# Keys and queries of steps 14 to 23: block transposes on VectorE and a pass through DRAM instead of TensorE transposes

## The chip, the cores and the metric

The kernel runs on one core of a Trainium2 chip. The core has five engines with a queue of their own, each of which works through its instructions in order: TensorE (PE in the profile; PEld is its weight load), VectorE (DVE), ScalarE (ACT), GpSimd (POOL) and SyncE (SP), which here only issues DMA transfers. ScalarE can issue DMA transfers too. An engine waits for another, or for a transfer, by a semaphore; while it waits, everything behind in its queue waits as well. The metric is the device time of one execution in microseconds (us), the median of several runs.

## The reference

A delta-rule attention over 4 batches, 8 heads, 768 tokens and head width 48 feeds a feed-forward block with a hard-swish. All inputs and the output are float32.

```python
k_n = k / (np.linalg.norm(k, axis=-1, keepdims=True) + 1e-06)
state = np.zeros((B, H, D, D), dtype=np.float32)
for t in range(S):
    kt, vt, bt = (k_n[:, :, t], v[:, :, t], beta[:, :, t, None])
    y[:, :, t] = np.einsum('bhd,bhde->bhe', q[:, :, t], state)
    v_old = np.einsum('bhde,bhd->bhe', state, kt)
    state = state + bt[:, :, :, None] * np.einsum('bhd,bhe->bhde', kt, vt - v_old)
...
x = np.ascontiguousarray(attn_out.transpose(0, 2, 1, 3)).reshape(B * S, H * D)
h = x @ w_in          # 3072 x 384 by 384 x 2048
g = h * np.clip(h + 3.0, 0.0, 6.0) / 6.0
return g @ w_out      # 3072 x 2048 by 2048 x 384
```

## The kernel before

The 768 tokens are cut into N = 24 steps of C = 32 tokens. In one step the four batches lie side by side on the 128 partitions (partition = 32 * batch + token), and the free dimension holds 8 heads of width 48, in some buffers padded to 64. Within a step the recurrence is solved as a triangular system: scores of keys against keys and queries (`sc`, L547), masked and scaled into `L` and `LB` (L558), an inverse of the triangular matrix worked out on VectorE for four steps at a time (`pr` and `A`, L759 and L764), and then the chain from step to step.

Two steps make a block of 256 tokens for the feed-forward. Its up and down products fill TensorE between the pieces of the recurrence. From block 5 on the up product is done with eleven partial products (`up_by_eleven`, L1066, its copies and sums at L1080, L1093, L1097, L1100, L1104 and L1107), before that plainly (L994, L1001, L1004). From block 2 on the down product is done with seven (`down_by_seven`, L1218, with sums of g on VectorE at L1204). In the part of the run that the change touches, odd steps are mostly filled with down products and even steps with up products.

The order is written by the program itself, in emission order for every engine. The first steps follow a list of words. From step 5 on a loop goes over steps t, each cut into 15 units u = 0 to 14. In each unit it calls the entry of `plan` for that unit, two key loads if there are any, one piece of the feed-forward (`units`), and as many instructions of `fill` (the inverse, the norms) as `room` allows; `room` subtracts from 1.65 us what VectorE has to do in that unit (`USED`, `CHAIN`). `take(gen)` advances a generator to its next bare `yield`.

Names that matter:

- `prep(t)` makes ready what the scores of step t need. GpSimd writes the normalised key into `kb` (L510). TensorE transposes four 128 x 128 pieces of it into PSUM (`pt`, L524) and ScalarE copies them into `KQ` (L532); the same for the query `qb`. Then come the 64 score matmuls (L547), and VectorE writes `L` and `LB` (L558). From t = 7 on the loop prepares `first_of` = t + 6: GpSimd's product is emitted at unit 13 of the step before (`later`), then the key's transposes at unit 1, the query's at unit 2, scores at unit 4, masks and `LB` at unit 5 (`now`).
- `KQ` holds for one step both operands with the head width on the partitions: head pair member e and width d on partition 64 * e + d, and in the free dimension the head pair and batch pair, four places y (key, query, query, key) and 32 tokens. There are NKQ = 6 of these buffers, 4 KB on each partition. A `KQ` is read by the scores and, six steps later, by the matmuls against the state (`ks`, L806).
- `chain(t)` is the recurrence: `ks` (L806) at unit 0, `R` (L901, L909), the product with the inverse (`pz`, L827), the update `su` (L938) and `py` (L827) at unit 8, the addition `y += py` (L863) and the new state (L956) at unit 9, and the transposes `yt` of y (L873) with ScalarE's copy into `xT` (L877) at unit 10. The up product of the block reads `xT`, after the sums at L1056 where it is done with eleven products.
- `load_q`, `load_k`, `load_v` issue four transfers of 48 KB on SyncE for one step; `to_dram` stores the output. Queries have NQB = 4 buffers, keys `kb` two.

Of the kernel before, what the change touches and what calls it, by code (L numbers as in the profile page):

```python
# [9 lines left out]
FP32 = mybir.dt.float32  # L10
# [34 lines left out]
def kernel(  # L45
# [49 lines left out]
    def rows(b):  # L95
        return slice(C * b, C * b + C)
# [24 lines left out]
    qbufs = [persist.tile([P, H, DP], FP32, name=f"qb{i}") for i in range(NQB)]  # L121
    bkbufs = [bkb_spare] + [
        persist.tile([P, H, DP], FP32, name=f"bkb{i}") for i in range(1, NBKB)
    ]
# [1 line left out]
    def bkb_of(t):  # L126
        return bkbufs[t if t < NBKB else 1 + (t - 1) % (NBKB - 1)]
# [3 lines left out]
    def tokens(ap, b, t):  # L131
        return ap[b, :, t * C : (t + 1) * C, :].rearrange("h t d -> t h d")
# [4 lines left out]
    def needs(*what):  # L137
        assert past.issuperset(what), (what, set(what) - past)
# [33 lines left out]

    def load_q(t, eng=nc.sync):
        if t < N:
            if t >= NQB:
                needs(("qT", t - NQB))
            elif t:
                needs(*pad(t))
            for b in range(B):
                eng.dma_start(out=qbufs[t % NQB][rows(b), :, 0:D], in_=tokens(q, b, t))  # L180
                if b == B - 1:
                    past.add(("q", t))
                yield
# [310 lines left out]
    def scaled(t):  # L494
        needs(("kb", t), *pad(t), *([("bkb", t - NKB)] if t >= NKB else []))
        if t >= NBKB:
            needs(("su", t - NBKB + 1))
        nc.gpsimd.tensor_tensor(
            out=bkb_of(t)[:, :, 0:D], in0=kbufs[t % NKB][:, :, 0:D],
            in1=beta_tok[:, t, 0:H].unsqueeze(2).to_broadcast([P, H, D]), op=ALU.mult,  # L500
        )
        past.add(("bkb", t))
        yield

    def prep(t, whole=True):

        g, i = group(t)
        kb, qb = kbufs[t % NKB], qbufs[t % NQB]
        needs(*([("bkb", t - NKB)] if t >= NKB else []), *(pad(t) if t < NKB and t else []))
        nc.gpsimd.tensor_tensor(  # L510
            out=kb[:, :, 0:D], in0=kfs[g][:, i],
            in1=invs.pop(t).unsqueeze(2).to_broadcast([P, H, D]), op=ALU.mult,
        )
        past.add(("kb", t))
        yield

        for j, src in enumerate((kb, qb)):
            if j == 1:
                needs(("q", t))
                past.add(("qT", t))  # L520
            ring("pm", NPM, ("pt", t, j))
            pt = psM.tile([128, NP, P], FP32, name="pt", tag=slot["pm"])
            for p in range(NP):
                nc.tensor.transpose(  # L524
                    pt[:, p, :], src[:, 2 * p : 2 * p + 2].rearrange("p e w -> p (e w)"), ident[:]
                )
            yield 1
            if j == 0:
                ring("KQ", NKQ, ("KQ", t))
                KQ = work.tile([128, NP * B // 2, 4, C], FP32, name="KQ", bufs=NKQ)  # L530
            read(("pt", t, j))
            nc.scalar.activation(  # L532
                out=KQ[:, :, 0:4:3, :] if j == 0 else KQ[:, :, 1:3, :],
                in_=pt[:].rearrange("q p (x y c) -> q (p x) y c", y=2, c=C), func=ACTF.Copy,
            )
            if whole and j == 0:
                drain(mask(t))
            yield
        ring("pc", NPC, ("sc", t))
        sc = psC.tile([P, 2, 512], FP32, name="sc", tag=slot["pc"])  # L540
        scv = sc[:, :, 0 : NP * 2 * C].rearrange("p e (a j w) -> p e a j w", a=NP, j=2)
        for p in range(NP):
# [24 lines left out]
        yield  # L567
# [219 lines left out]
    def chain(t, whole=True):  # L787
# [10 lines left out]
        def of_state():  # L798
            ph = [banks("ks", t, i) for i in range(2)]
            for p in range(NP):  # L800
                for b in (0, 2, 1, 3):
                    for e in range(2):
                        r = slice(DP * e, DP * e + DP)
# [622 lines left out]
    with tc.manual_schedule():  # L1426
# [11 lines left out]
        loads = iter(())  # L1438
        left = due = 0
        USED = {"up": 0.42, "eleven": 1.0, "down": 0.7}  # L1440
        CHAIN = {0: 0.45, 1: 0.75, 2: 0.75, 3: 0.4, 4: 0.4, 6: 0.5, 9: 0.8, 10: 0.6, 14: 0.2}
        for t in range(LS, N):
            g, i = group(t)
# [9 lines left out]
            if i == 2:  # L1453
# [12 lines left out]
                11: lambda: token_sums(t // CB),  # L1466
                13: lambda: take(later),
            }
            if behind:
                for u in (7, 8, 10, 11, 12, 13):  # L1470
                    plan[u] = lambda ch=plan.get(u): (ch and u < 13 and ch(), take(more))
                plan[14] = lambda: take(later)
            ready = (2, 0) if behind or i == 2 and t - LS == LA - LE else (1, 6)
            for u in range(NU):
                if u in plan:
                    plan[u]()
                take(loads, 2)
# [24 lines left out]
                left, due = max(left - int(due), 0), due - int(due)  # L1502
# [33 lines left out]
```

## Time and profile before

| what | value |
|---|---|
| median of 3 runs | 665.78 us (665.2 to 667.13) |
| profiled execution, its own time | 672.08 us |
| its span | 670.4 us |
| granted TensorE clock, mean | 0.985 |
| first `ks` of steps 7, 8 and 18, from the span's start | 214.84, 240.44, 493.37 us |
| transposes `pt` (L524) | 192 in 48 groups, 24 of key and 24 of query; the last at 472.8 us |
| copies into `KQ` (L532) | 48, 576 to 608 ns each |

How to read the lines that follow: the page gives busy time and share of each engine, then the chain of work that ended last. A row of the table by stretches gives the stretch in us, its length, the busy time of each engine with its number of instructions, the granted clock, the share of the DMA engines and GB/s. A row of the timeline gives start, length from the first start to the last end, engine, line, operation, tile written <- tiles read, shapes and count; in brackets the idle time before it and what ended it. A row of the groups gives the count, busy us and mean ns of one, and the idle time before. A row of the DMA issues gives the count, the size and the median time from issue to landing.

### The profile page before, as it was taken

Reading aid. Unit: us, or ns where it says so; the run is one execution under the profiler, and the core shown is the slowest. Engines: PE = TensorE matmul, PEld = TensorE weight load, DVE = VectorE, ACT = ScalarE, POOL = GpSimd, SP = SyncE. Lnnn points to the kernel's source line nnn. Section 1 sums busy time; section 2 is a strip of 40 time slices with the busy share of each in tenths; the row PEclk is TensorE's granted clock in tenths of the full one; section 3 lists DMA queues with packets and bytes.
Section 4 is the critical chain, followed back from the end, with each engine's and each line's share of the span. In section 5 each row is a group of like instructions: output and inputs, shape, how many; then the busy total and the mean of one; then the engine's idle time right before and its main releaser. Section 6 shows DMA issues by size and latency. Waiting matters only on the chain.

```text
span 670.4 us, 26330 instructions
## 1 busy us (share of the span) xinstructions
PE 636.9 (95%) x11544; PEld 568.6 (85%) x11544; DVE 487.2 (73%) x1146; ACT 272.8 (41%) x532; POOL 203.6 (30%) x320
## 2 busy tenths in 40 slices
PE   2768899999999999999999999999999999999997
PEld 2657786776688988988989999999999999999997
DVE  4889685899545777747879847988748988556354
ACT  5887568532142232232234234235244144153250
POOL 5531022002421031364155255055042141331330
PEclk9959899999999999999999999999999999999999
DMA  7888237302041030032030020020020020010000
GB/s 171 203 193 235 59 67 186 73 6 51 15 80 32 2 72 2 3 73 37 3 68 8 3 61 14 3 62 2 3 50 2 2 49 2 17 24 2 25 1 25
DMA packets 88499, 33.27 MB, mean 50 GB/s; under 512 B 80160, under 2 KB 83232, under 8 KB 88384
## 3 DMA queue, kind: packets, MB, share of 16 engines
q1 hardware_dynamic: 88128, 31.29, 20.7%
q8 instruction: 91, 1.49, 0.9%
q10 hardware_dynamic: 256, 0.30, 0.2%
q14 instruction: 24, 0.20, 0.1%
HBM read 26.84 MB, written 4.72 MB: 47 GB/s over the span
## 4 chain that ended last, share of the span: by engine, by line
PE 86%; DMA 5%; DVE 3%; SPq 2%; issue 1%; ACT 1%; POOL 0%; ACTq 0%; DVEq 0%; POOLq 0%
PE po L1218 28%; PE ph L1066 20%; PE ph L994 15%; PE po L1154 6%; PE ks L806 3%; PE su L938 3%; PE pz L827 3%; PE py L827 3%; PE pt L524 2%; PE sc L547 2%; DMA spare<-in_moe_w_in_dram 2%; DMA kf<-in_k_dram 1%; PE yt L873 1%; DMA w_out<-in_moe_w_in_dram 1%; PE pi L684 1%
## 5 line engine op out<-in xcount | busy, mean ns | idle before, releaser
L1066 PE MATMUL ph<-xT,w_in 128*128 128x128 f32 (+1 forms) x560 | 121.4, 321 | 0.8 <-ACT KQ L532 0.6
L994 PE MATMUL ph<-xT,w_in 128*128 128x256 f32 (+1 forms) x576 | 116.6, 351 | 2.9 <-DVE g L1004 2.1
L1218 PE MATMUL po<-w_out,g 128*128 128x192 f32 x640 | 110.6, 326 | 0.0
L994 PEld LDWEIGHTS ph<-xT,w_in 128*128 128x128 f32 x576 | 94.5, 192 | 15.8 <-DVE g L1004 2.9
L1218 PEld LDWEIGHTS po<-w_out,g 128*128 128x128 f32 x640 | 104.6, 190 | 0.5
L1066 PEld LDWEIGHTS ph<-xT,w_in 128*128 128x128 f32 x560 | 91.1, 191 | 6.0 <-ACT KQ L532 0.8
L1030 POOL TENSOR_TENSOR g<-g 128x256 f32<-128x256 f32 x112 | 68.0, 608 | 83.2 <-ACT g L1080 78.8
L1218 PE MATMUL po<-spare,g 128*128 128x192 f32 x480 | 86.7, 332 | 0.0
L1218 PEld LDWEIGHTS po<-spare,g 128*128 128x128 f32 x480 | 77.2, 190 | 1.8
L1001 ACT ACTIVATE g<-ph,halves 128x256 f32<-128x256 f32 (+1 forms) x96 | 41.3, 436 | 74.9 <-PE ph L994 74.8
L1080 ACT ACTIVATE g<-ph 128x512 f32<-128x512 f32 x56 | 33.4, 597 | 82.1 <-PE ph L1066 82.1
L1228 POOL TENSOR_TENSOR o<-o,u 128x192 f32<-128x192 f32 x18 | 13.2, 733 | 175.7 <-ACT o L1225 97.2
L1204 DVE TENSOR_TENSOR g<-g 128x512 f32<-128x512 f32 x80 | 55.6, 716 | 5.6 <-PE po L1218 5.6
L759 DVE TENSOR_TENSOR pr<-A 128x30 f32<-128x30 f32 (+9 forms) x150 | 57.4, 383 | 2.8
L764 DVE TENSOR_TENSOR A<-A,pr 128x30 f32<-128x30 f32 (+9 forms) x150 | 55.7, 371 | 3.7
L1004 DVE SCALAR_TENSOR_TENSOR g<-g,ph 128x256 f32<-128x256 f32 (+1 forms) x96 | 34.8, 371 | 31.7 <-ACT g L1001 31.4
L356 ACT ACTIVATE spare<-spare,places 128x768 uint16<-128x768 uint16 (+1 forms) x56 | 52.4, 942 | 2.7 <-DMA kf<-in_k_dram 1.5
L1093 DVE TENSOR_TENSOR g<-ph,g 128x256 f32<-128x256 f32 x56 | 23.5, 420 | 38.4 <-PE ph L1066 30.9
L1225 ACT ACTIVATE o<-po 128x192 f32<-128x192 f32 x40 | 13.2, 330 | 83.2 <-PE po L1218 79.6
L510 POOL TENSOR_TENSOR kb<-kf,inv 128x384 f32<-128x384 f32 x24 | 21.3, 891 | 78.8 <-issue 42.6
L1154 PE MATMUL po<-w_out,g 128*128 128x384 f32 x128 | 45.2, 491 | 0.0
L1107 DVE SCALAR_TENSOR_TENSOR g<-o,g 128x512 f32<-128x512 f32 x56 | 40.7, 726 | 5.9 <-ACT o L1104 5.9
(141 smaller groups left out, 1010.6 us busy)
## 6 DMA issues: line engine op xcount, KB each, us to landing
kf<-in_k_dram SPq DMA_DIRECT2D x96, 48.0 KB, 2.9
qb<-in_q_dram SPq DMA_DIRECT2D x96, 48.0 KB, 2.8
vf<-in_v_dram SPq DMA_DIRECT2D x96, 48.0 KB, 2.2
out_dram<-o SPq DMA_DIRECT2D x92, 48.0 KB, 1.6
spare<-in_moe_w_in_dram SPq DMA_DIRECT2D x4, 768.0 KB, 6.0
w_out<-in_moe_w_in_dram SPq DMA_DIRECT2D x4, 768.0 KB, 6.5
w_out<-in_moe_w_out_dram SPq DMA_DIRECT2D x4, 768.0 KB, 7.3
spare<-in_moe_w_out_dram SPq DMA_DIRECT2D x4, 768.0 KB, 5.7
```

Of the source, the lines that this page charges most:

```text
L356: nc.scalar.activation(out=z, in_=z if n else d.bitcast(I16)[:, :, :, 3], func=func, bias=places[:, n : n + 1], scale=scale,)
L759: nc.vector.tensor_tensor(out=pv, in0=A[:, j + 1 :, j].unsqueeze(2).to_broadcast([n, w, j]), in1=A[:, j, 0:j].unsqueeze(1).to_broadcast([n ...
L764: nc.vector.tensor_tensor(out=A[:, j + 1 :, 0:j], in0=A[:, j + 1 :, 0:j], in1=pv, op=ALU.subtract)
L827: nc.tensor.matmul(ps[rows(place(b)), D * h : D * h + D], lhsT=m(h)[rows(b)], rhs=z[rows(b), D * at(h) : D * at(h) + D], start=True, stop= ...
L994: nc.tensor.matmul(ph[:, cols], lhsT=w_in[:, s, f * 128 : (f + 1) * 128], rhs=xT[:, s, cols], start=(s == 0), stop=(s == NKT - 1),)
L1001: nc.scalar.activation(out=g, in_=ph, func=ACTF.Relu, bias=half, scale=1.0 / 6.0)
L1030: nc.gpsimd.tensor_tensor(out=out, in0=a, in1=b, op=op)
L1066: nc.tensor.matmul(ph[:, n], lhsT=w, rhs=x, start=start, stop=stop, skip_group_check=True)
L1107: nc.vector.scalar_tensor_tensor(out=g, in0=r, scalar=1.0, in1=g, op0=ALU.min, op1=ALU.mult)
L1154: nc.tensor.matmul(pos[c][:], lhsT=gs[blk, f // 2][:, f % 2, c * P : (c + 1) * P], rhs=w_out[:, f, :], start=(f == 0), stop=(f == NFC - 1),)
L1204: nc.vector.tensor_tensor(out=A(f, *out, 4), in0=A(f, *a, 4), in1=A(f, *b, 4), op=op)
L1218: nc.tensor.matmul(ps[n][:], lhsT=A(f - f % 2, *a)[:, f % 2], rhs=b[:, f], start=(f == 0), stop=(f == HF - 1),)
```

## The change

For the steps from TQ = LS + 2 * LE + 1 = 14 on, `prep` uses no TensorE. VectorE transposes the 128 x 384 query in blocks of 32 x 32 into a buffer `turned`; SyncE writes it with four transfers, one for each batch, into a tile `kq` in DRAM (384 rows of head and width; two such tiles). The key follows in the same way, through the same `turned`. Then ScalarE issues two transfers that read `kq` into `KQ`, one for the even and one for the odd heads, in runs of 1 KB. The scores and `ks` read 48 of the 64 partitions of each half.

`KQ` becomes a ring of fixed slots. Six are the buffers of before; step 14 and every seventh step after it use a slot cut from the area of the four query buffers, which also holds `turned` and the one query buffer of the late steps (`late_q`). A late query can therefore be loaded only after the query before it has been turned.

In the loop, GpSimd's product and the query's turn are emitted at unit 7 of the step before, the key's turn at unit 8, the reads into `KQ` at unit 12. The masks stay at unit 1, the scores at unit 4. The entries at units 2 and 6 no longer advance `prep`. `room` subtracts 0.6 us more in units 7 and 8.

```diff
+    TQ = LS + 2 * LE + 1
+    q_area = persist.tile([P, NQB * H * DP], FP32, name="qb")
...
+    KQW = 4 * C * NP * B // 2
+    late_kq = q_area[:, 0:KQW].rearrange("p (a y c) -> p a y c", y=4, c=C)
+    turned = q_area[:, KQW : KQW + H * D]
+    late_q = q_area[:, KQW + H * D : KQW + 2 * H * D].rearrange("p (h w) -> p h w", w=D)
+    early_kq = [
+        persist.tile([128, NP * B // 2, 4, C], FP32, name=f"KQ{i}") for i in range(NKQ)
+    ]
+
+    def kq_slot(t):
+        return t % NKQ if t < TQ else NKQ if t == TQ else kq_slot(t - NKQ - 1)
...
     def load_q(t, eng=nc.sync):
         if t < N:
-            if t >= NQB:
-                needs(("qT", t - NQB))
+            if t > TQ:
+                needs(("qT", t - 1))
+            elif t >= NQB:
+                needs(*(("qT", t - NQB + n) for n in range(2 if t == TQ else 1)))
...
+        def turn_by_blocks(j):
+            nc.vector.transpose(
+                out=turned, in_=(of_query if j else of_key)(t).rearrange("p h w -> p (h w)")
+            )
+            for b in range(B):
+                nc.sync.dma_start(
+                    out=kq[:, b // 2, (2 if j else 3) if b % 2 else j, :].rearrange(
+                        "(n r) c -> r n c", r=C
+                    ),
+                    in_=turned[rows(b)].rearrange("p (n c) -> p n c", c=C),
+                )
+
+        if t >= TQ:
+            kq = scratch.tile([H * D, B // 2, 4, C], FP32, name="kq", bufs=2)
+            needs(("q", t))
+            turn_by_blocks(1)
+            past.add(("qT", t))
+            yield
+            turn_by_blocks(0)
+            yield
+            KQ = kq_of(t)
...
+            for e in range(2):
+                nc.scalar.dma_start(
+                    out=KQ[DP * e : DP * e + D].rearrange("d (p x) y c -> d p (x y c)", p=NP),
+                    in_=kq[:].rearrange("(p e d) x y c -> e d p (x y c)", e=2, d=D)[e],
+                )
+            yield
+            drain(mask(t))
+        yield
+
+        for j, src in enumerate((kb, qb) if t < TQ else ()):
...
-                    r = slice(DP * e, DP * e + DP)
+                    r = slice(DP * e, DP * e + (DP if t < TQ else D))
...
+        TURN = {7: 0.6, 8: 0.6}
...
+            if first_of >= TQ:
+                plan[2] = lambda: (take(ch), take(gens["q"], 4))
+                plan[6] = lambda: None
+            if first_of + 1 >= TQ:
+                plan[7] = lambda: take(later)
+                plan[8] = lambda: (take(ch), take(later))
+                plan[12] = lambda: take(later)
+                plan[13] = lambda: None
...
+            turns = TURN if first_of + 1 >= TQ else {}
...
-                room = max(1.65 - USED[mode["of"]] - CHAIN.get(u, 0), 0.15) / mode["mean"]
+                room = max(1.65 - USED[mode["of"]] - CHAIN.get(u, 0) - turns.get(u, 0), 0.15) / mode["mean"]
```

More of the change, by code (lines that the diff above doesn't have):

```diff
@@ L120, with kq_of, of_key, of_query @@
     kbufs = [persist.tile([P, H, DP], FP32, name=f"kb{i}") for i in range(NKB)]
-    qbufs = [persist.tile([P, H, DP], FP32, name=f"qb{i}") for i in range(NQB)]
+    TQ = LS + 2 * LE + 1
+    q_area = persist.tile([P, NQB * H * DP], FP32, name="qb")
+    qbufs = [
+        q_area[:, i * H * DP : (i + 1) * H * DP].rearrange("p (h w) -> p h w", w=DP)
+        for i in range(NQB)
+    ]
[5 more added lines that the diff above has]
+        persist.tile([128, NP * B // 2, 4, C], FP32, name=f"KQ{i}") for i in range(NKQ)
+    ]
+    def kq_slot(t):
+        return t % NKQ if t < TQ else NKQ if t == TQ else kq_slot(t - NKQ - 1)
+    def kq_of(t):
+        i = kq_slot(t)
+        return late_kq if i == NKQ else early_kq[i][:]
+    def of_key(t):
+        x = kbufs[t % NKB][:]
+        if t < TQ:
+            return x[:, :, 0:D]
+        return x.rearrange("p h w -> p (h w)")[:, 0 : H * D].rearrange("p (h w) -> p h w", w=D)
+    def of_query(t):
+        return qbufs[t % NQB][:, :, 0:D] if t < TQ else late_q
     bkbufs = [bkb_spare] + [
@@ L179, in load_q @@
             for b in range(B):
-                eng.dma_start(out=qbufs[t % NQB][rows(b), :, 0:D], in_=tokens(q, b, t))
+                eng.dma_start(out=of_query(t)[rows(b)], in_=tokens(q, b, t))
                 if b == B - 1:
@@ L498, in scaled @@
         nc.gpsimd.tensor_tensor(
-            out=bkb_of(t)[:, :, 0:D], in0=kbufs[t % NKB][:, :, 0:D],
+            out=bkb_of(t)[:, :, 0:D], in0=of_key(t),
             in1=beta_tok[:, t, 0:H].unsqueeze(2).to_broadcast([P, H, D]), op=ALU.mult,
@@ L510, in prep @@
         nc.gpsimd.tensor_tensor(
-            out=kb[:, :, 0:D], in0=kfs[g][:, i],
+            out=of_key(t), in0=kfs[g][:, i],
             in1=invs.pop(t).unsqueeze(2).to_broadcast([P, H, D]), op=ALU.mult,
@@ L514, in prep @@
         past.add(("kb", t))
+        def turn_by_blocks(j):
[18 more added lines that the diff above has]
+            KQ = kq_of(t)
+            needs(("read", ("KQ", max(s for s in range(t) if kq_slot(s) == kq_slot(t))))
+                  if t > TQ else ("qT", t - 1))
+            for e in range(2):
[5 more added lines that the diff above has]
+            drain(mask(t))
         yield
-        for j, src in enumerate((kb, qb)):
+        for j, src in enumerate((kb, qb) if t < TQ else ()):
             if j == 1:
@@ L528, in prep @@
             if j == 0:
-                ring("KQ", NKQ, ("KQ", t))
-                KQ = work.tile([128, NP * B // 2, 4, C], FP32, name="KQ", bufs=NKQ)
+                if t >= NKQ:
+                    needs(("read", ("KQ", t - NKQ)))
+                KQ = kq_of(t)
             read(("pt", t, j))
@@ L802, in of_state @@
                     for e in range(2):
-                        r = slice(DP * e, DP * e + DP)
+                        r = slice(DP * e, DP * e + (DP if t < TQ else D))
                         c = slice(2 * C * (b // 2), 2 * C * (b // 2) + 2 * C)
```

## The prediction

> **What bounds the kernel now.** I read the page's busy shares and chain of waits first, then busy times by stage, then the timeline of one engine at a time. The page says TensorE:
>
> ```profile
> span 670.4 us, 26330 instructions
> PE 636.9 (95%) x11544; PEld 568.6 (85%) x11544; DVE 487.2 (73%) x1146; ACT 272.8 (41%) x532; POOL 203.6 (30%) x320
> ...
> PE 86%; DMA 5%; DVE 3%; SPq 2%; issue 1%; ACT 1%; POOL 0%; ACTq 0%; DVEq 0%; POOLq 0%
> ```
>
> A share is a mean, so I cut the span at the first `ks` matmul (L806) of each step. Steps 11, 12, 17, 18 and 19:
>
> ```profile
> core 0: us, PE busy (x) PEld busy (x) DVE busy (x) ACT busy (x) POOL busy (x), PEclk, DMA share, GB/s
> ...
> 317.12:342.21 25.09, 25.09 (x455) 23.86 (x454) 21.35 (x47) 5.49 (x12) 6.72 (x10) 1.00 0.04 12
> 342.21:367.99 25.78, 25.18 (x466) 22.81 (x465) 22.07 (x52) 12.62 (x26) 14.44 (x22) 1.00 0.20 40
> ...
> 468.28:493.37 25.09, 25.09 (x454) 23.86 (x454) 15.71 (x34) 6.21 (x13) 4.71 (x8) 1.00 0.04 12
> 493.37:516.51 23.14, 23.14 (x395) 21.35 (x394) 16.25 (x40) 12.37 (x25) 7.81 (x14) 1.00 0.13 26
> 516.51:539.93 23.42, 23.42 (x383) 22.33 (x382) 21.78 (x52) 4.30 (x10) 5.38 (x8) 1.00 0.05 13
> ```
>
> TensorE is busy in practically every microsecond of these steps. So whatever is taken out of its queue is saved, and whatever it is made to wait is lost. VectorE is loaded unevenly: 16 us in some steps, 22 of 25 in others.
>
> **What is removed.** Steps 8 to 17 each hold two groups of four transposes (`pt`, L524) for steps 14 to 23. In step 11:
>
> ```profile
> 318.20 1.57 PE L1218 MATMUL po<-spare,g 128*128 128x192 f32 x8
> ...
> 319.44 0.52 PEld L524 LDWEIGHTS pt<-ident,kb 128*128 128x128 f32 x4
> ...
> 319.93 1.28 PEld L1218 LDWEIGHTS po<-spare,g 128*128 128x128 f32 x8
> ...
> 321.18 0.52 PEld L524 LDWEIGHTS pt<-ident,qb 128*128 128x128 f32 x4
> ...
> 321.67 2.58 PEld L1218 LDWEIGHTS po<-w_out,g 128*128 128x128 f32 x16
> ```
>
> A group keeps the queue from 319.44 to 319.93, 0.49 us (321.18 to 321.67 again). 20 groups x 0.49 = 9.8 us. Cross-check: steps 18 and 19, with neither transposes nor scores, are 1.7 to 1.95 us shorter than step 17; two groups and the 0.86 us of scores make 1.84. The one TensorE wait for a `KQ` copy after step 7 (0.6 us, L1066, at 347.45) goes too: 10.4 us saved. The 20 ScalarE copies (L532, 0.6 us each) go, off the path. The score and `ks` matmuls read 48 rows instead of 64; the score group (64 rows) and `py` (32 rows) both last about 0.9 us, so I take 0.
>
> **What is added, where covered.** SyncE issues 80 more transfers at a pitch of 0.47 us (v loads start at 292.18, 292.65, 293.14), 38 us on a queue that waits 329.6 us for GpSimd's `o`. A query load now waits for the previous query's turn, a step earlier; in step 12 such loads go out at 345.8 to 347.8 and take 2.8 us, 7 us before the turn. GpSimd's `kb` product moves from unit 13 to unit 7 and is done before the key's turn, which waits for more (below). ScalarE issues the two reads into `KQ` at unit 12: in step 11, by the working below, the key's writes land at 339.1, ScalarE issues until about 340.0, and its next copy is due at 342.0 (339.83 before, plus the 2.2 us by which TensorE is late). The reads land by 342.9; the scores come at 351. Cover 2 and 8 us; were the first gone, the copy (L1080), on which TensorE's second accumulation waits, would be late by the excess.
>
> **What is added on the path.** VectorE turns the query (Q) at unit 7 and the key (K) at unit 8, into the one buffer `turned`. Hence K waits until Q's four writes to DRAM have landed, and VectorE's queue is in order: behind K stand the g sums, some inverse work and `y+=py` (L863), and TensorE's next instruction but a few is the transpose of that y (`yt`, L873). The rows:
>
> ```profile
> L255 DVE STREAM_TRANSPOSE beta_tok<-spare 128x768 f32<-128x768 f32 x1 | 1.0, 970 | 0.0
> L612 DVE STREAM_TRANSPOSE sums_in<-sums_in 128x256 f32<-128x256 f32 x1 | 0.4, 446 | 0.0
> ```
>
> ```profile
> q1 hardware_dynamic: 88128, 31.29, 20.7%
> ...
> kf<-in_k_dram SPq DMA_DIRECT2D x96, 48.0 KB, 2.9
> qb<-in_q_dram SPq DMA_DIRECT2D x96, 48.0 KB, 2.8
> vf<-in_v_dram SPq DMA_DIRECT2D x96, 48.0 KB, 2.2
> out_dram<-o SPq DMA_DIRECT2D x92, 48.0 KB, 1.6
> ```
>
> A turn of 384 columns lies between 446 ns (256) and 970 (768): 0.57 us. The four issues start 0.05 to 1.45 us after Q. A write of 48 KB into DRAM by 384 pieces of 128 B is not in the trace; nearest are 1.6 us (a store of 32 long rows) and 2.2 to 2.9 (loads of 256 pieces of 192 B). I take 2.0, as a store with many pieces; 1.6 and 2.9 bound it. Below 1.6 there is no row: the store already has few pieces, so I allow no gain there.
>
> So from Q's start to a finished `y` are 0.57 (Q) + 1.45 + 2.0 + 0.57 (K) + 0.55 (L863) + 0.1 (hand-over) = 5.24 us plus what stands between K and L863. Step 12 in the timeline:
>
> ```profile
> 357.50 0.33 DVE L759 TENSOR_TENSOR pr<-A 128x168 f32<-128x168 f32 x1
> ...
> 360.29 0.55 DVE L863 TENSOR_TENSOR y<-y,py 128x384 f32<-128x384 f32 x1
> ...
> 360.98 0.52 PE L873 MATMUL yt<-ident,y 128*128 128x128 f32 x3
> ```
>
> By the changed program's order Q stands behind the product at 357.50, so it starts at 357.8; between K and L863 is one product (0.33). y is ready at 363.4, `yt` stood at 360.98: 2.4 us late. The same in each step (Q's start; work between; `yt` before; late):
>
> - 7: 226.95; 0.99; 233.53; 0
> - 8: 254.0; 1.2; 259.07; 1.4
> - 9: 279.04; 1.24; 284.67; 0.85
> - 10: 305.24; 0.66; 310.21; 0.93
> - 11: 331.1; 1.49; 335.64; 2.2
> - 12: 357.8; 0.33; 360.98; 2.4
> - 13: 380.97; 0.69; 386.68; 0.25
> - 14: 408.06; 0.2; 411.23; 2.3
> - 15: 432.55; 1.05; 436.90; 1.95
> - 16: 457.7; 0.33; 461.27; 2.0
>
> Sum 14.3 us; with 1.6 us to land 10.8, with 2.9 22.9. The two turns' own time (20 x 0.57 = 11.4 us) is in these sums; otherwise it replaces inverse work, which is spread over units. Where VectorE has a backlog, Q does not move up with TensorE: up to 0.98 more in steps 11 and 15, inside the upper bound.
>
> **Sum.** -10.4 + 14.3 = +3.9 us (+0.4 to +12.5). The profiled execution has a span of 670.4 and a time of 672.08, so it would become 676.0; it stands 6.3 us above the median of 665.78, a difference I carry over unchanged, as nothing before step 7 is edited: 669.7 (666.2 to 678.3).
>
> **Rivals.** Hidden wait, the faster side: VectorE gets to Q earlier than the old times say. Every stall of TensorE lets VectorE work off its backlog, and fewer inverse steps stand in units 7 and 8. The price is 1 us per us in nine steps, and it decides from 0.4 us per step on (14.3 against 10.4). With half the lateness gone 665.8 - 10.4 + 7.1 = 662.5; with all gone 655.4. For it: step 7, where VectorE is ahead, is not late; against: VectorE has 22 us to do in half of the steps.
>
> Draw: lateness about 10 us, as at the lower landing bound, 666; no change.
>
> Slow small writes: a turn's four writes are 1536 pieces, 96 per DMA engine; the mean piece on q1 costs 0.207 x 16 x 670.4 / 88128 = 25 ns, so 2.4 us per turn, about the issue time. If pieces of 128 B cost double, the engines need 4.8 us, and K starts some 2.5 us later in each step: 669.7 + 24 = 694. Against it: the 192 B loads land in 2.2 us.
>
> [...]
>
> That the transposes stay is excluded: no `pt` of steps 14 to 23 is in the changed program's order.
>
> **How the numbers follow.** Stall as worked out 0.43, hidden wait 0.30, draw 0.13, slow writes 0.14. No change means within 0.3% (663.8 to 667.8), about what a measurement of this kernel tells apart. Faster: 0.28 of the hidden wait. Same: the draw, 0.02 of the hidden wait, 0.05 of the forecast's low end: 0.20. Slower: 0.38 + 0.14 = 0.52. The forecast's own range is 666 to 678; 658 to 684 takes in most of the hidden wait and leaves out slow writes.
>
> **What would show it.** Right: K (second turn of a step) waiting 2 to 3 us for a write of `kq`; `yt` idle for VectorE's y 0.3 to 2.4 us in steps 8 to 16; steps 8 to 16 at 24.4 to 26.6 us, step 17 at 24.1. Wrong: TensorE without a wait in those steps, each 24.1 us; writes landing under 1.6 or over 2.9 us; or ScalarE's `KQ` reads, not `yt`, ending TensorE's waits.

## The result, and the profile after

The changed kernel takes 699.09 us in the median of 4 runs (696.24 to 699.88), the kernel before beside it 665.49 us: a ratio of 1.0492, 95% interval 1.0457 to 1.0527. The prediction was 669.7 us with a range of 658 to 684; the time lies outside it, on the side that was forecast. The profiled execution took 699.88 us.

The page of the changed kernel, busy shares and chain of waits:

```profile
span 697.8 us, 26284 instructions
PE 640.4 (92%) x11464; PEld 569.9 (82%) x11464; DVE 494.3 (71%) x1166; ACT 261.4 (37%) x512; POOL 202.3 (29%) x320
...
PE 63%; DVE 14%; issue 8%; DMA 6%; ACT 5%; SPq 2%; POOL 2%; DVEq 0%; ACTq 0%; POOLq 0%
```

Eighty transposes are gone, and yet TensorE is busy for 3.5 us longer than before (640.4 against 636.9): some of its matmuls ran slower (`po`, 128x192: 524 ns each between 344.14 and 350.97 us, where the granted clock was 0.5; 326 ns in steps 7 to 17 before). In the chain it fell from 86% to 63%; VectorE rose from 3% to 14%.

Steps 11, 12, 17, 18 and 19, cut at the first `ks` matmul of a step as before (columns: stretch; its length; busy time and instructions of each engine; granted clock; DMA share; GB/s):

```profile
core 0: us, PE busy (x) PEld busy (x) DVE busy (x) ACT busy (x) POOL busy (x), PEclk, DMA share, GB/s
324.09:354.30 30.21, 27.37 (x446) 25.94 (x445) 22.53 (x49) 4.30 (x10) 7.69 (x11) 0.89 0.31 63
354.30:382.71 28.41, 25.77 (x458) 23.41 (x458) 21.36 (x51) 12.11 (x25) 13.75 (x21) 0.94 0.28 52
492.07:519.77 27.70, 25.68 (x446) 24.33 (x446) 16.86 (x39) 5.15 (x12) 4.72 (x8) 0.94 0.07 16
519.77:542.90 23.13, 23.13 (x394) 21.34 (x393) 15.72 (x37) 12.37 (x25) 7.82 (x14) 1.00 0.13 27
542.90:566.33 23.43, 23.43 (x383) 22.34 (x382) 20.94 (x51) 4.30 (x10) 4.99 (x8) 1.00 0.05 12
```

Step 11 went from 25.09 to 30.21 us, step 17 from 25.09 to 27.70; steps 18 and 19 stand where they stood. TensorE, without a gap before, now idles for 2.84 of the 30.21 us, and the clock granted in the step is 0.89. In these two traces the loss lies in steps 7 to 17, which take 308.4 us where they took 278.5.

What TensorE and VectorE waited for between 200 and 700 us (engine, what it ran and its line, what released it; us in total, times, longest):

```profile
PE yt L935 <- DVE y L925: 21.9, 10, 2.8
PE pz L889 <- DVE X L503: 4.1, 3, 2.0
PE pz L889 <- ACT y L905: 0.7, 1, 0.7
```

```profile
DVE g L1155 <- PE ph L1128: 37.2, 27, 2.8
DVE qb L547 <- DMA kq<-qb: 31.5, 10, 4.4
```

This is the predicted chain: in all ten steps the key's turn waits for a write of `kq` (the row `qb L547`: the profile calls the buffer `turned` by the name of its area, `qb`), and `yt` then waits for y. The second TensorE row, the inverse `X` late for `pz`, was not predicted.

VectorE and one TensorE row in step 12, the step that the prediction worked out (start, duration, instruction, in brackets the idle time before it):

```profile
372.64 0.58 DVE L547 STREAM_TRANSPOSE qb<-kb 128x384 f32<-128x384 f32 x1 [1.92 <-DMA kq<-qb]
373.15 0.29 DVE L821 TENSOR_TENSOR pr<-A 128x168 f32<-128x168 f32 x1
373.36 0.55 DVE L925 TENSOR_TENSOR y<-y,py 128x384 f32<-128x384 f32 x1
```

```profile
374.05 0.52 PE L935 MATMUL yt<-ident,y 128*128 128x128 f32 x3 [2.65 <-DVE y L925]
```

The query's turn ended at 369.23, so the key's started 3.41 us after it (predicted 3.45). Between the key's turn and `y += py` stands one product, as predicted, and TensorE is idle for 2.65 us ahead of `yt` (predicted 2.4). Step 8 is another matter:

```profile
257.24 0.58 DVE L547 STREAM_TRANSPOSE qb<-kb 128x384 f32<-128x384 f32 x1 [4.29 <-DMA kq<-qb]
```

Here the query's turn ended at 251.91 and the key's started 5.33 us after it. In steps 7 to 16 this wait from turn to turn was 5.20, 5.33, 4.95, 4.77, 4.70, 3.41, 3.36, 3.54, 4.88 and 3.39 us: four steps as predicted, six by 1.3 to 1.9 us longer. The DMA queues in exactly that wait, first of step 8, then of step 12 (queue and kind; packets, MB, share of the 16 engines):

```profile
q1 hardware_dynamic: 1600, 0.20, 24.4%
q8 instruction: 1, 0.02, 1.8%
issues: line engine op xcount, KB each, median us to landing
kq<-qb SPq DMA_DIRECT2D x4, 48.0 KB, 2.8
```

```profile
q1 hardware_dynamic: 1600, 0.20, 38.2%
issues: line engine op xcount, KB each, median us to landing
kq<-qb SPq DMA_DIRECT2D x4, 48.0 KB, 1.8
```

In the long wait there is also one packet of 16 KB of the kind `instruction` (queue q8), an instruction fetch in what follows, and one of the four writes, issued 1.42 us behind the query's turn, landed 5.21 us behind it. The section on the prediction returns to it.

Last, the clock. Two neighbouring windows of 3.41 us (in these traces the granted clock changes only at multiples of that) around the idle time of step 8, and two around that of step 15:

```profile
255.40:258.81 3.41, 1.17 (x6) 0.68 (x4) 1.54 (x5) 0.86 (x2) 0.00 (x0) 1.00 0.04 5
258.81:262.22 3.41, 2.85 (x9) 2.41 (x10) 3.34 (x10) 0.49 (x1) 0.00 (x0) 0.50 0.58 94
453.37:456.78 3.41, 1.52 (x10) 1.23 (x8) 1.14 (x3) 0.00 (x0) 0.00 (x0) 1.00 0.10 13
456.78:460.20 3.42, 2.48 (x17) 2.52 (x18) 3.38 (x10) 0.49 (x1) 0.90 (x2) 1.00 0.37 58
```

The idle time ahead of `yt` in step 8 is 2.80 us. TensorE was idle for 2.24 us of the first window (3.41 - 1.17), and the next ran at half clock. In step 15 an idle time of nearly the same length, 2.82 us, fell across the edge of two windows, 1.88 us of it in the first, and the clock stayed full. Steps 7 to 17 hold 23.9 us at half clock; in the kernel before there was none between 76 us and the last 0.3 us.

So the 29.9 us come from: idle time of TensorE 26.7 (before 0.8), half clock at most 12.0 (an estimate: half of 23.9, as if TensorE were busy throughout; 16 `po` matmuls of 128x192 kept it busy for 5.3 us at half clock between 344.14 and 350.97 us, 0.33 us each, 49 of them between 211.35 and 258 us, at full clock, for 8.6, 0.18 each), less 8.0 us of work saved. Sum: 25.9 + 12.0 - 8.0 = 29.9. The 8.0 are what the other two leave over, so they carry the error of the 12.0.

### The profile page after: what moved, and what is told of

It is laid out like the page before. It is cut to its first block, busy times and chain, and to the rows that moved or that the text cites. A ratio compares the mean times of both kernels' runs of the same rounds, so it can differ in the third digit from the quotient of the medians.

```text
span 697.8 us, 26284 instructions
## 1 busy us (share of the span) xinstructions
PE 640.4 (92%) x11464; PEld 569.9 (82%) x11464; DVE 494.3 (71%) x1166; ACT 261.4 (37%) x512; POOL 202.3 (29%) x320
## 4 chain that ended last, share of the span: by engine, by line
PE 63%; DVE 14%; issue 8%; DMA 6%; ACT 5%; SPq 2%; POOL 2%; DVEq 0%; ACTq 0%; POOLq 0%
PE ph L1128 16%; PE po L1280 15%; PE ph L1056 13%; PE po L1216 5%; DMA kq<-qb 4%; PE ks L868 3%; ACT spare L386 3%; PE pz L889 2%; DVE g L1266 2%; PE su L1000 2%; SPq L551 2%; PE pt L585 2%; DMA kf<-in_k_dram 2%; DVE g L1169 1%; DVE A L826 1%
## 5 line engine op out<-in xcount | busy, mean ns | idle before, releaser
L1128 PE MATMUL ph<-xT,w_in 128*128 128x128 f32 (+1 forms) x560 | 123.3, 326 | 0.5 <-ACT g L1142 0.4
L1280 PE MATMUL po<-w_out,g 128*128 128x192 f32 x640 | 114.8, 334 | 0.0
L1280 PEld LDWEIGHTS po<-w_out,g 128*128 128x128 f32 x640 | 109.0, 196 | 0.5
L1056 PEld LDWEIGHTS ph<-xT,w_in 128*128 128x128 f32 x576 | 96.8, 196 | 14.2 <-ACT xT L939 1.0
L1128 PEld LDWEIGHTS ph<-xT,w_in 128*128 128x128 f32 x560 | 93.6, 195 | 6.7 <-ACT g L1142 0.6
L826 DVE TENSOR_TENSOR A<-A,pr 128x30 f32<-128x30 f32 (+9 forms) x150 | 53.8, 358 | 2.9
L1166 ACT ACTIVATE o<-g,halves 128x512 f32<-128x512 f32 x56 | 40.5, 723 | 9.3 <-DVE g L1169 5.4
```

The source lines that it names most:

```text
L826: nc.vector.tensor_tensor(out=A[:, j + 1 :, 0:j], in0=A[:, j + 1 :, 0:j], in1=pv, op=ALU.subtract)
L1056: nc.tensor.matmul(ph[:, cols], lhsT=w_in[:, s, f * 128 : (f + 1) * 128], rhs=xT[:, s, cols], start=(s == 0), stop=(s == NKT - 1),)
L1128: nc.tensor.matmul(ph[:, n], lhsT=w, rhs=x, start=start, stop=stop, skip_group_check=True)
L1166: nc.scalar.activation(out=r, in_=g, func=ACTF.Relu, bias=half, scale=1.0 / 6.0)
L1280: nc.tensor.matmul(ps[n][:], lhsT=A(f - f % 2, *a)[:, f % 2], rhs=b[:, f], start=(f == 0), stop=(f == HF - 1),)
```

## The experiments

Eleven kernels were run (e1 to e12; there is no e5). The ratio is that to the kernel before on the same chip in the same session, with its 95% interval. The columns behind it are read from each one's trace in steps 7 to 17: length; TensorE idle ahead of `yt`, and idle ahead of `pz`; time at half clock; and what is left when all idle time and half of the time at half clock are taken off.

| kernel | median us | ratio | 7 to 17 | idle `yt` | idle `pz` | half | left |
|---|---|---|---|---|---|---|---|
| before | 665.49 | 1 | 278.5 | 0 | 0 | 0 | 277.8 |
| changed | 699.09 | 1.0492 (1.0457 to 1.0527) | 308.4 | 21.9 | 4.3 | 23.9 | 269.8 |
| e1_two_buffers | 672.43 | 1.0056 (1.0020 to 1.0091) | 278.0 | 1.5 | 5.7 | 3.4 | 269.1 |
| e2_before_one_buffer | 703.39 | 1.0523 (1.0451 to 1.0595) | 313.7 | 22.1 | 1.5 | 17.1 | 279.3 |
| e3_before_two_buffers | 672.47 | 1.0075 (1.0037 to 1.0112) | 282.7 | 0.8 | 2.1 | 0 | 278.5 |
| e4_key_behind_y | 678.79 | 1.0155 (1.0093 to 1.0218) | 285.7 | 2.6 | 4.4 | 3.4 | 270.7 |
| e6_two_buffers_no_reserve | 664.76 | 0.9958 (0.9931 to 0.9984) | 275.6 | 4.6 | 0.7 | 0 | 269.8 |
| e7_two_buffers_inverse_early | 664.99 | 0.9978 (0.9948 to 1.0008) | 275.8 | 4.4 | 1.0 | 0 | 269.9 |
| e8_no_turn_on_vectore | 661.53 | 0.9901 (0.9865 to 0.9937) | 272.3 | 2.4 | 0.7 | 0 | 269.1 |
| e9_key_behind_y_reads_14 | 671.24 | 1.0067 (1.0042 to 1.0093) | 284.2 | 1.2 | 6.0 | 10.2 | 269.0 |
| e10_one_buffer_key_behind_y | 676.90 | 1.0144 (1.0099 to 1.0189) | 285.5 | 2.4 | 6.4 | 6.8 | 269.7 |
| e11_no_inverse_before_y | 666.53 | 0.9980 (0.9946 to 1.0013) | 274.3 | 0 | 3.3 | 0 | 269.7 |
| e12_one_buffer_no_reserve | 694.34 | 1.0413 (1.0369 to 1.0458) | 303.1 | 23.2 | 1.6 | 13.7 | 271.1 |

The last column falls into two families: 278 to 279 with the TensorE transposes, 269 to 271 without. So by this account the transposes were worth 7 to 9 us in every kernel, and all else is idle time and clock. Outside steps 7 to 17 the profiled executions differ in the start of the kernel, which no edit touches: the first `ks` of step 7 stands between 209.4 and 217.2 us. That is why a stretch is compared as well as a time.

### Is it the one buffer? (e1, e2, e3, e4)

e1 gives the two turns a buffer each (the key's lies where the late query lay):

```diff
-    turned = q_area[:, KQW : KQW + H * D]
+    turneds = [q_area[:, KQW + i * H * D : KQW + (i + 1) * H * D] for i in (1, 0)]
...
         def turn_by_blocks(j):
+            turned = turneds[j]
```

> The key's turn writes into the area of the late query (free once the query is turned), so it no longer waits for the query's four writes; all else as in the changed kernel. Theory A (the loss is the key's turn waiting for the one buffer, TensorE idling at yt behind it, and the clock halving after such idle times): no wait of VectorE for writes of kq, no idle time over 0.5 us before yt, no half clock between steps 7 and 18, and the 9.8 to 10.4 us of transposes come through: 654 to 659 us, faster than before. Theory B (VectorE is overloaded by the 11.4 us of turns, whatever it waits for): little change against the changed kernel, 690 to 700. Theory C (the path through DRAM is late for the scores, or ScalarE is blocked at its reads of kq): 690 to 700 too, with the waits moved to sc or to ScalarE.

e2 and e3 are the kernel before, TensorE transposes and all, with the two turns of a constant and their eight unread writes added in steps 7 to 16 (late queries use two of the four query buffers, to make room); e2 through one buffer, e3 through two:

```diff
+    def turn_by_blocks(j):
+        turned = turneds[j]
+        nc.vector.transpose(out=turned, in_=w_in[:, 1, 0 : H * D])
+        for b in range(B):
+            nc.sync.dma_start(
...
+                plan[7] = lambda: turn_by_blocks(1)
+                plan[8] = lambda: (take(ch), turn_by_blocks(0))
```

> The kernel before keeps its TensorE transposes, and in steps 7 to 16 VectorE also makes two turns of a constant at units 7 and 8, through one buffer, each written to DRAM by four transfers that nothing reads (two query buffers serve the late steps). Theory A: the same waits as in the changed kernel without its 10 us of saving: yt idle 2 to 3 us in most of the ten steps, half clock after several, 700 to 712 us. Theory B: the two turns' own time shows alike here and with two buffers. Theory C (the reads of kq or the scores): nothing of it is here, 666 to 672.

> As the run with one buffer, but query and key are turned into two buffers. Theory A: VectorE waits for no write; only the 11.4 us of turns are added to an engine with room: 665 to 669 us. Theory B: as with one buffer, 695 to 712. If the many small writes themselves slow the loads or TensorE, it lies between.

e4 leaves the one buffer and puts the key's turn at unit 9, behind `y += py` and the state:

```diff
-                plan[8] = lambda: (take(ch), take(later))
+                plan[9] = lambda: (take(ch), take(later))
...
-        TURN = {7: 0.6, 8: 0.6}
+        TURN = {7: 0.6, 9: 0.6}
```

> The changed kernel with its one buffer, but the key's turn is emitted at unit 9 behind y+=py and the new state, not at unit 8 ahead of them. Theory A: VectorE still waits some 1 to 3 us for the writes in each step, but yt no longer stands behind that wait: TensorE's idle times before yt go, the clock stays full, 655 to 665 us. If it is the wait of VectorE as such that costs (all its later work late), 680 to 700.

One buffer against two settles most of it. With two the wait for y falls from 21.9 to 1.5 us (e1), and one buffer brings the same 22 us of waiting into the kernel before (e2), where nothing reads what is written. What VectorE waited for in e2:

```profile
DVE g L1093 <- PE ph L1066: 34.0, 24, 2.8
DVE qb L1332 <- DMA kq<-qb: 33.2, 10, 4.5
```

e3, where no work is saved and no write is waited for, still costs 0.75%, 672.5 us where 665 to 669 were expected: the 20 turns (11.4 us of VectorE), with their writes and the 0.6 us set aside for each, are not free. And e1 is not the 654 to 659 us that were expected; e4 missed its 655 to 665 as well. In e1 the work is saved and given away again; its TensorE waits:

```profile
PE pz L890 <- DVE X L503: 4.2, 3, 2.1
PE pz L890 <- DVE R L972: 1.8, 2, 1.4
PE yt L936 <- DVE y L926: 1.5, 2, 0.8
```

e4 loses time elsewhere. In its trace ScalarE comes to its reads into `KQ` at unit 12 before the key's writes have landed: it idles ahead of them in seven of the ten steps, 21.0 us in all (5.4 us in five steps of the changed kernel), and `ph` then waits 2.7 us for its copies. `R` is late as well (3.8 us at `pz`).

### What makes the inverse late? (e6, e7, e8)

The planner subtracts 0.6 us in units 7 and 8 (`TURN`) from the room for the inverse, but divides by the same mean room as before, so it plans fewer instructions than it has. The rest falls in one lump behind the group's last y, ahead of `X`: in VectorE's order 9 and 10 inverse instructions in the kernel before for its `X` at 371 and 471 us, 13 and 15 in e1 for those at 372 and 473. VectorE in e1, at the end of that lump:

```profile
372.00 0.18 DVE L827 TENSOR_TENSOR A<-A,pr 128x30 f32<-128x30 f32 x1
372.17 0.09 DVE L831 MEMSET A<- 128x32 f32 x1
372.29 1.94 DVE L503 STREAM_TRANSPOSE X<-A 128x1024 f32<-128x1024 f32 x1
```

The last products run in the same stretch as `R` and the `g` sums. The transpose `X`, 1.94 us, ends at 374.23, the second part of `R`, which stands behind it in the queue, at 374.63, and the next `pz`, at 374.78, has waited 1.43 us for that `R`. e6 is e1 without the set-aside:

```diff
-        TURN = {7: 0.6, 8: 0.6}
+        TURN = {}
```

> The changed kernel with two buffers for the turns (as e1_two_buffers) and without the 0.6 us that the plan sets aside in units 7 and 8 for a turn, so that as many steps of the inverse stand in those units as before the change. Theory C (in e1_two_buffers the set-aside moved 3 to 4 inverse instructions of each group behind the group's last y, X came late, and TensorE waited 7.2 us for it and for what stands behind it): the idle time of TensorE in steps 7 to 16 falls from 7.2 us to 1 to 3, no half clock there, 6 to 8 us under the kernel before, 657.5 to 661. Rival D (VectorE has no room for the 11.4 us of turns wherever they stand): y+=py gets late in place of X, TensorE waits 5 us or more for y, and the time stays at 668 to 674.

e7 also takes the inverse earlier:

```diff
-                room = max(1.65 - USED[mode["of"]] - CHAIN.get(u, 0) - turns.get(u, 0), 0.15) / mode["mean"]
+                room = max(1.65 - USED[mode["of"]] - CHAIN.get(u, 0) - turns.get(u, 0), 0.15) / (mode["mean"] / 1.3)
```

> As e6_two_buffers_no_reserve, and the plan takes the inverse 1.3 times as early, so that 6 or 7 inverse instructions are left behind a group's last y, where it was 13 to 15 in e1_two_buffers and 9 or 10 in the kernel before. Theory C: no wait for X in steps 8 to 16, 656 to 660. Rival D: waits for y and R of 5 us or more in all, 668 to 675.

e8 is e6 without the turns themselves:

```diff
-            turned = turneds[j]
-            nc.vector.transpose(
-                out=turned, in_=(of_query if j else of_key)(t).rearrange("p h w -> p (h w)")
-            )
+            turned = (of_query if j else of_key)(t).rearrange("p h w -> p (h w)")
```

> As e6_two_buffers_no_reserve without the 20 turns on VectorE: the writes take keys and queries as they lie, so the scores are made from rows that were not transposed; all transfers and the rest stay. C and D both: no wait of TensorE beyond the kernel before's, 8.7 to 10.4 us under it, 656 to 658.5. If it stays above 662, it is not VectorE that eats the gain but the transfers, ScalarE's reads or the clock (rival E).

e6 ends the wait for `X`, and the half clock with it; its TensorE waits are:

```profile
PE yt L936 <- DVE y L926: 4.6, 3, 1.7
PE pz L890 <- DVE R L972: 0.4, 1, 0.4
...
PE pz L890 <- DVE X L503: 0.2, 1, 0.2
```

It is the one kernel with the turns whose interval lies below 1: 0.4% faster than the kernel before, 0.9931 to 0.9984. This is less than theory C gave it (657.5 to 661), since 3 us of waits for y came back, as rival D says, and less time than D gave it (668 to 674). e7, with 6 to 7 instructions left in the lump, gains nothing over it and lies between its two expectations. e8 shows what VectorE's 11.4 us of turns still cost: 272.3 against 275.6 us in the stretch, 3.3 us. With all transfers in place and no turn the time is 661.5; that excludes the transfers, ScalarE's reads and the clock (rival E) as what holds e6 back by more than a few us, though the time is 6.0 us under the kernel before beside it (667.5) and not the 8.7 to 10.4 that both theories gave: TensorE still idles for 3.1 us, 2.4 of them ahead of `yt` in steps 12 and 16, where no turn can be the cause.

A part of that is probably GpSimd's. The change also moved its key product from unit 13, behind `y += py`, to unit 7, ahead of it, and in e8 it runs over products of the inverse:

```profile
353.58 0.94 POOL L540 TENSOR_TENSOR kb<-kf,inv 128x384 f32<-128x384 f32 x1
```

```profile
353.86 0.84 DVE L819 TENSOR_TENSOR pr<-A 128x168 f32<-128x168 f32 x1
```

The same VectorE product took 0.33 us in the kernel before, at 357.50, with GpSimd idle. In steps 12 and 16 of e8 two products under the GpSimd product lose some 0.65 us together, of the 1.2 us that `yt` waits in each of these steps, and e6 has the same overlap. No run leaves the GpSimd product at unit 13, so what the move costs in all is open.

### Is there room on VectorE at all? (e9, e10, e11)

e9 has two buffers, the key's turn behind y, ScalarE's reads two units later, and the inverse early; e10 is the same without the two lines on `turneds`. Both keep 0.6 us set aside in units 7 and 9, but only in the steps that hold turns (in the changed kernel it goes on to the last step), and there divide the mean room by 1.3 to make up for it:

```diff
+    turneds = [q_area[:, KQW + i * H * D : KQW + (i + 1) * H * D] for i in (1, 0)]
...
+            turned = turneds[j]
...
-                plan[8] = lambda: (take(ch), take(later))
-                plan[12] = lambda: take(later)
+                plan[9] = lambda: (take(ch), take(later))
...
+                plan[14] = lambda ch=plan.get(14): (ch and ch(), take(later))
...
-            turns = TURN if first_of + 1 >= TQ else {}
+            turns = TURN if TQ <= first_of + 1 < N else {}
```

> Two buffers, the key's turn at unit 9 behind y+=py and the state's update, ScalarE's reads into KQ at unit 14 in place of 12, and the plan takes the inverse 1.3 times as early, so that 9 or 10 of its instructions are left behind a group's last y, as before the change. If the 4.6 us that TensorE still waits for y in e6_two_buffers_no_reserve come from the two turns standing ahead of y (theory F), they fall to 1.5 us or less and the time is 658 to 662. If VectorE is simply behind in the steps with the eleven-row g's (rival G), the wait for y or for R stays at 4 us or more, 664 to 667. If the later reads come too late for the scores, TensorE waits for KQ and it is 668 or more.

> As e9_key_behind_y_reads_14, but with the one buffer of the changed kernel, so the key's turn waits for the query's four writes, now behind y. Theory A (the wait costs what is queued behind the key's turn and is needed soon): the wait of 1 to 3 us stays on VectorE, TensorE does not wait for y, and it is within 2 us of e9_key_behind_y_reads_14, 30 us or more under the changed kernel. If one buffer costs in itself, whatever stands behind it, 680 or more. In e4_key_behind_y the reads at unit 12 held ScalarE by some 20 us; with unit 14 this goes, and the time is 10 us or more under that run.

```profile
PE pz L890 <- DVE R L972: 5.5, 6, 1.7
PE sc L610 <- issue: 2.1, 1, 2.1
PE yt L936 <- DVE y L926: 1.2, 1, 1.2
```

These are e9's TensorE waits. Theory F is right in that the wait for y falls to 1.2 us, and wrong in the time: `R` is late instead, by 5.5 us, with 10.2 us at half clock behind these waits and the one at `sc`, and the time is above rival G's range too. The 2.1 us at `sc` (in e4 and e10 too) have no releaser in the profile. In all three kernels they lie behind the 57th of the 64 score matmuls in step 17, and in e9 the reads into `KQ` had landed 3 us before the first of these, so it is not the late `KQ` of the third expectation; what it is stays open. e10 says what a buffer costs when its wait is put where little is due: VectorE's wait for `kq` shrinks from 31.5 us to 5.3, and the kernel is some 22 us under the changed one with the same buffer, where 30 were expected. It is not within 2 us of e9 by the medians (5.7 us), though it is by the stretch (285.5 against 284.2); the rest is not explained. Nor is it 10 us under e4, but 1.9 us, although ScalarE's idle time ahead of the reads fell from 21.0 to 1.3 us: little of e4's time seems to hang on that.

e11 takes all inverse instructions of the eleven-row steps out of units 6 to 9:

```diff
+                if turns and mode["of"] == "eleven" and 6 <= u <= 9:
+                    continue
```

with the inverse 2.2 times as early elsewhere.

> As e6_two_buffers_no_reserve, but in the steps with the eleven-row g's no inverse instruction stands in units 6 to 9, so nothing of it lies ahead of y+=py there, and the plan takes it 2.2 times as early elsewhere, so that 7 to 11 instructions are left behind a group's last y. If VectorE's order decides (theory C carried on), the 4.6 us that TensorE waits for y in e6_two_buffers_no_reserve fall below 2.5 us, and the time is 1 to 4 us under that run: 660 to 664. If VectorE is simply full there (rival D), what is taken from y comes back as waits for R and X, and the time is 664 to 668.

```profile
PE pz L890 <- DVE R L972: 3.3, 3, 1.3
PE ph L1129 <- DVE xT L1119: 0.7, 2, 0.4
```

The wait for y is gone, and 3.3 us of waits for `R` stand in its place. The stretch is 1.3 us shorter than e6's; the time (666.5, in rival D's range) can't be told from it. What one reader of VectorE gains, another loses: most of what rival D says holds, VectorE has no room to spare in these steps.

### The fourth corner (e12)

The changed kernel with its one buffer, and `TURN = {}`:

> The changed kernel with its one buffer, and without the 0.6 us set aside in units 7 and 8: the fourth corner beside the changed kernel (699), e1_two_buffers (672) and e6_two_buffers_no_reserve (665). If the two causes add up (theory A plus C): 689 to 694, with waits of about 22 us for y and of 1 us for X. If most of the changed kernel's loss were the late inverse, it would be near e6_two_buffers_no_reserve, 665 to 675. If the inverse instructions back in units 7 and 8 stand behind the waiting turn of the key, y gets later still and the wait for y grows: 694 to 700.

Its TensorE waits:

```profile
PE yt L935 <- DVE y L925: 23.2, 10, 3.7
PE pz L889 <- DVE R L971: 1.3, 2, 0.9
...
PE pz L889 <- DVE X L503: 0.2, 1, 0.2
```

| ratio to before | set-aside | none |
|---|---|---|
| one buffer | 1.0492 | 1.0413 |
| two buffers | 1.0056 | 0.9958 |

The two causes add up: the buffer is worth 4.4 to 4.6 per cent of the time before, the set-aside 0.8 to 1.0, whichever way one goes, and the interval of each ratio is 0.3 to 0.5 per cent to either side. The time, 694.3 us, lies on the border of the first and the third expectation: the wait for y grew by 1.3 us, as the third said it would in direction, and the wait for `X` went, as the first said. In the two traces with one buffer most of the difference is half clock (23.9 against 13.7 us), which depends on where the idle times fall on the windows (2.80 us of idle time in step 8 of the changed kernel stand ahead of a window at half clock, 2.82 us in step 15 ahead of none), so the 0.8 rests on the medians alone.

## Why the prediction was wrong

**Right: the mechanism and its place.** A turn takes 568 ns (query) and 578 ns (key) in the median (0.57 us predicted); the four issues stand 0.03 to 1.42 us behind the query's turn in nine of ten steps (0.05 to 1.45); VectorE's in-order queue carries the wait to y and `yt` (in step 12 1.92 us of idle time ahead of the key's turn, 2.65 ahead of `yt`). In steps 12, 13 and 14 `yt` waits 2.65, 0.48 and 2.26 us where 2.4, 0.25 and 2.3 were forecast. e2 and e3 show that one buffer in place of two, without the rest of the change, costs 4.5% (1.0523 against 1.0075), what it costs here.

**The step that failed: a microsecond of idle TensorE was priced at one microsecond, and the clock was put at nothing.** The prediction said that "whatever it is made to wait is lost", and its sum, -10.4 + 14.3 = +3.9 us, has no other price for a wait. Steps 7 to 17 took 29.9 us more, 26.0 over the sum. The terms: up to 12.0 us are half clock behind the idle times, nearly half as much again as the idle time itself; 7.6 are a longer idle time ahead of `yt` (21.9 against 14.3); 4.3 are idle ahead of `pz`; 1.6 were not saved; the rest is small. The idle time ahead of `yt` lies inside the forecast's own bounds (10.8 to 22.9). With every term but the clock put right the sum gives some 684 us, the end of the stated range, and with the clock some 696. The 3 us from there to the median can't be assigned: the profiled execution stands 6.3 us above its median before the change and 0.8 us after it. That idle time brings half clock is shown both ways: with two buffers both shrink (e1: 7.2 us idle, 3.4 at half clock), and with one both come into the kernel before (e2: 25.8 and 17.1).

**A term that was too small: "2.0 us to land", and the lateness of 14.3 us made from it.** In the four steps in whose wait no instruction fetch begins, the key's turn starts about 2.0 us behind the last write's issue (3.41 - 1.42 in step 12). In the other six one of the four writes takes longer. The wait between the turns is 4.35 us in the mean and not 3.45, 9 us more in ten steps. In the three kernels that wait at unit 8 (changed, e2, e12) there are 30 such waits: 18 with a 16 KB instruction fetch that begins in them, all of 4.3 to 5.3 us, and 12 without, all of 3.4 to 3.9. It is not that a longer wait catches more fetches: all 18 begin within the first 3.1 us. The traces of the changed kernel and the experiments hold the landing of 480 writes of `kq`: 162 took over 2.1 us, and 161 of these had a fetch in flight; of the other 318, 62 had one. (In the changed kernel alone: 40 writes, 11 over 2.1 us, all 11 with a fetch; of the other 29, 4.) No run took the fetches away, so that they cause it is read from this coincidence and not shown. The bound of 2.9 us was the largest loading row; the longest write of the changed kernel took 3.9.

**"Otherwise it replaces inverse work, which is spread over units": wrong.** The turns' time is subtracted from the plan in two units and not given back, so that the inverse piles up ahead of `X`: 3.0 of the 4.3 us ahead of `pz` are waits for `X` here, and between e1 and e6 the set-aside is worth 1.0%, some 6.5 us.

**10.4 us saved: a little too much.** Steps without a wait are 0.88 us shorter (25.54 to 24.66, e1 and e6), that is 0.44 for a group of four and not 0.49; 8.0 us of work are gone in the changed kernel, 7 to 9 over all runs without the transposes, and with them 0.8 us of waits that the kernel before had: 8.8 and not 10.4.

**Cover.** That ScalarE's reads cost TensorE nothing was right: no TensorE wait names `KQ`. The cover of 2 us ahead of them was not there in all steps: in steps 7, 9, 11, 13 and 15 ScalarE idles for 0.1 to 2.8 us until the key's writes have landed.

**The rivals.** The hidden wait fell: VectorE did not get ahead of the wait in any step. Slow small writes named a time near the result (694), by luck and not by cause: the writes' median is 1.8 us beside 1.6 for the stores with their 1536 B rows, and in the waits without an instruction fetch all is as forecast. No run shows pieces of 128 B at double cost: in the wait of step 12 the 1600 packets of a turn's four writes took 0.382 x 16 x 3.41 us / 1600 = 13 ns in the mean, where the prediction worked out 25 ns for the mean piece on q1 and the rival doubled it. In the best order found, moving the transposes off a full TensorE wins 0.4%, since the turns on VectorE take back 3.3 us (e6 against e8).

## What to carry to other kernels

A single staging buffer between an engine and a DMA puts the write's whole latency, issue pitch included, into the engine's in-order queue (3.36 to 5.33 us from turn to turn here); count what stands behind the second use, and take the slowest of the writes (3.9 us here) and not their median (1.8). Time set aside in a hand-made plan must be given back elsewhere in the plan, or the work it displaces piles up at the deadline (13 and 15 inverse instructions ahead of `X` in e1, 9 and 10 before). And on a TensorE that never idled, a stall of 2.1 us inside one window of 3.41 us can cost up to 3.8, an estimate (2.1 and half of the next 3.41), since the clock fell to 0.5 behind every window here with 2.07 us or more of idle time; a gain of 9 us on one full engine is only had if the engine that takes over the work has the room at that point of its order.

## What the hardware showed

**Half clock behind 2.07 us and more of idle time.** In all traces, TensorE's granted clock changes only at multiples of 3.41 us on a grid that is fixed within an execution. Steps 7 to 17 of all traces hold 15 such windows with 2.07 us or more of idle time, and all 15 were followed by a half-clock window (five each in the changed kernel and e2, four in e12, one in e4). From 1.45 to 2.03 us it went either way (7 with, 12 without); what decides there, perhaps the small matmuls in the busy part, is open. The least of the 15 was idle for 61% of its 3.41 us; in the changed kernel the five were idle for 2.08 to 2.61 us.

**Small writes.** 48 KB into DRAM in 384 pieces of 128 B land in 1.8 us (changed kernel, median; 1.6 to 3.9), beside 1.6 us for stores of the same size in rows of 1536 B; the medians of eight experiments are 1.8 (e2), 1.9 (e10, e12), 2.1 (e6, e9), 2.2 (e4) and 2.9 us (e1, e8). Of the 162 that took over 2.1 us, 161 had an instruction fetch of 8 or 16 KB in flight. A wait for four such writes ends with the last of them (step 8: the last landing known at 5.21 us behind the query's turn, the key's turn at 5.33).

**VectorE products under GpSimd.** In the kernel before, between 200 and 600 us, the 55 inverse instructions of 184 to 234 columns that no GpSimd instruction overlaps take 0.34 to 0.41 us; of the 31 that lie for 60% or more of their time under GpSimd instructions, 25 take 0.53 to 0.91 and the other six 0.36 to 0.40.
